# Three copies of split heads made by DMA, and the last sums completed block by block of tokens

## The chip, the cores and the metric

The kernel runs on one core of a Trainium2 chip. The metric is device time in microseconds (us) of one execution, as the median of several runs. The names of the engines are those of the profile: PE is TensorE (PEld its weight loads), DVE is VectorE, ACT is ScalarE, POOL is GpSimd, SP is SyncE, whose queue issues all the DMAs here. A name such as L233 is a line of the kernel before.

## The reference

Inputs are q, k, v of 8 batches x 8 heads x 576 tokens x 64 in float32, a memory matrix M_prev (64 x 64) and a vector z_prev (64) for each head, a gate beta for each head, and the weights of a feed-forward layer, 512 x 2048 and 2048 x 512. What is computed:

```python
scores = q @ k.T / sqrt(64)           # causal mask, 576 x 576 for each head
a = softmax(scores)
local = a @ v
q_p = elu(q) + 1
mem_out = (q_p @ M_prev) / (q_p . z_prev + 1e-6)
x = sigmoid(beta) * mem_out + (1 - sigmoid(beta)) * local
h = x.reshape(4608, 512) @ w_in
out = (h * sigmoid(h)) @ w_out        # 4608 x 512, float32
```

## The kernel before

**Precision.** A float32 number is split into a rounded part (type fp32r) and the rest ("high" and "low"), and a product is made as high x high + high x low + low x high in fp32r matmuls. The first ten heads (`N_WHOLE`) are "whole" instead: their attention runs in plain float32 matmuls. The other 54 heads are "split", and only these hold the three copies that the change touches.

**A head.** `scores` (from L215) transposes 64 channels of k and q together into `tt` (L221: k on partitions 0 to 63, q on 64 to 127). In a split head the two operands of the score product are built so that one pass over 128 partitions makes two terms:

- `kk`: rounded k above (L230, ACT), its rest below (L232, POOL).
- `qq`: rounded q on partitions 64 to 127 (L231, ACT) and once more on partitions 0 to 63 (L233, ACT); `ql` and 64 further columns of `qq` hold the rest of q (L235, POOL).
- L237 (ACT) repeats the last 64 columns of rounded q, on all 128 partitions, in 64 columns at the end of `qq`. They serve the second half of the last row of blocks (L274), which takes the columns S to S + 127 of `qq`.

The five blocks of 128 queries then follow: the score matmuls (L250; L274 for the last, of 64 queries in two halves), mask and minimum on DVE (L252, L284), the exponential on ACT (L254, L294), sums, and the normalizing of the probabilities `p` on POOL (L304). L307 (POOL) copies a 64 x 64 piece of the last block's probabilities to 64 columns further right, on the same partitions. The second transpose of L393 in each head reads that piece.

`values` (from L337) runs one head later: it transposes the probabilities on PE (L376, L384, L393), splits them (`ph` on ACT at L406, `pl` on DVE at L407) and multiplies by v and by the memory (L414, L422); the result goes into `xt`.

**The feed-forward part.** `ffn` works on 18 units of 256 tokens. A unit runs through eight pairs of blocks of the inner dimension: products into `h` (L552), tanh and the gating (L563, L564), the split into `g` (L567, L569), and, one pair later, the second product into two sums `acc` of 128 tokens each (`second`, L525 to L536). Within `second` the loop over the two weight tiles of the pair is the outer one and the loop over the two blocks of tokens the inner one; a block takes three matmuls from each tile. After the last pair the sums are scaled by 0.5 on ACT (L579) and stored (L581).

**Weights.** Most weight tiles stay on the chip. Twelve of the 32 ("flow": four of the first matrix, eight of the second) are read again for each unit (L485) into a ring of two buffers. Of the last pair of a unit the first tile stays on the chip and the second is a flow tile.

**The order of the work.** The main loop steps the generators for attention, weight preparation and feed-forward in turn, so that feed-forward steps lie between attention steps. The framework's planner then writes each engine's order of instructions by simulating the program with its own durations. On the chip each engine, and each queue of DMAs, runs its list strictly in order. Buffers set how far a head may run ahead: `tt`, `kk`, `qq` and the probabilities have two each, `raw` has one.

Of the kernel before, what the change touches and what calls it, by code (L numbers as in the profile page):

```python
# [12 lines left out]
AF = mybir.ActivationFunctionType  # L13
ALU = mybir.AluOpType
# [26 lines left out]
def memory_attention_then_silu_ffn(ctx, tc, q, k, v, M_prev, z_prev, beta, w_in, w_out, out):  # L41
    nc = tc.nc
    B, H, S, D = q.shape
    NT, DM = out.shape
    DFF = w_in.shape[1]
    P = 128
    NQ = (S + P - 1) // P
    LAST = S - (NQ - 1) * P
    SPLIT = 2 * P
    HI = S - SPLIT  # L50
    T = 256
    NU = NT // T
    KD = DM // P
    KF = DFF // P
    NP = KF // 2
# [17 lines left out]
    def f(ap):  # L73
        return ap.bitcast(F32)
# [11 lines left out]
        out=mask[:, 3 * P:], in_=mask[:, 3 * P:], pattern=[[-1, P]], base=0, channel_multiplier=1,  # L86
# [128 lines left out]
    def scores(b, h, raw, rest, made, whole):  # L215
# [4 lines left out]
        tt = pool.tile([P, S], F32, tag="tt", name="tt", bufs=NB["tt"])  # L220
        anchor["dve"] = nc.vector.transpose(out=tt, in_=raw.rearrange("p c e -> p (c e)")).ins  # L221
        if whole:
            qq = pool.tile([P, S], F32, tag="kk", name="qf", bufs=QK_BUFS)
            nc.scalar.copy(qq[0:64], tt[64:P])
            terms = [(qq[0:64], tt[0:64])]
        else:
            kk = pool.tile([P, S], F32R, tag="kk", name="kk", bufs=QK_BUFS)
            qq = qrow[h % QK_BUFS]
            ql = qlow[h % QK_BUFS]
            nc.scalar.copy(kk[0:64], tt[0:64])  # L230
            nc.scalar.copy(qq[64:P, 0:S], tt[64:P])  # L231
            nc.gpsimd.tensor_tensor(out=kk[64:P], in0=tt[0:64], in1=f(kk[0:64]), op=ALU.subtract)  # L232
            nc.scalar.copy(qq[0:64, 0:S], tt[64:P])  # L233
            for low, x0, x1 in ((ql[0:64], 0, S - LAST), (qq[0:64, S:S + LAST], S - LAST, S)):
                nc.gpsimd.tensor_tensor(  # L235
                    out=low, in0=tt[64:P, x0:x1], in1=f(qq[64:P, x0:x1]), op=ALU.subtract)
            nc.scalar.copy(qq[:, S + LAST:], f(qq[:, S - LAST:S]))  # L237
            terms = [(qq, kk), (ql, kk)]
        yield

# [4 lines left out]
        for i in range(NQ - 1):  # L245
            w = P * i + P
            pt = pool.tile([P, w], F32, tag=f"p{i}", name=f"p{i}", bufs=P_BUFS)
# [14 lines left out]
        pt = pool.tile([P, 3 * P], F32, tag=f"p{i}", name=f"p{i}", bufs=P_BUFS)  # L262
        halves = []
        for side, other, x0, x1, o in ((slice(0, LAST), slice(LAST, P), 0, SPLIT, P),
# [7 lines left out]
            else:  # L272
# [3 lines left out]
                if x1 == S:  # L276
                    nc.gpsimd.tensor_tensor(
                        out=row[:, x1 - x0 - LAST:], in0=row[:, x1 - x0 - LAST:], in1=mask[side, 4 * P - LAST:],
# [8 lines left out]
        def halves_of(out, src, op):  # L287
# [12 lines left out]
            out=st[:, 15:15 + NQ], in0=st[:, 10:10 + NQ], scalar=1.0e-9, in1=over[:, 1, h],  # L300
            op0=ALU.add, op1=ALU.mult)
# [2 lines left out]
            nc.gpsimd.tensor_scalar(  # L304
                pb[x], pb[x], st[:, 15 + x:16 + x], 1.0, op0=ALU.mult, op1=ALU.mult)
        if not whole:
            nc.gpsimd.tensor_copy(pt[LAST:P, HI:], pt[LAST:P, HI - LAST:HI])  # L307
        yield


# [1 line left out]
        if not whole:  # L312
            a, c = (D, 0) if odd else (0, D)
# [15 lines left out]
            out=r, in0=e, in1=zb.rearrange("p (o d) -> p o d", o=1).to_broadcast([P, NQ, D]), op=ALU.mult)  # L329
        nc.vector.tensor_reduce(nrm, r, axis=AX.X, op=ALU.add)  # L330
        nc.vector.scalar_tensor_tensor(
            out=nrm, in0=nrm, scalar=1.0e-6, in1=over[:, 0, h], op0=ALU.add, op1=ALU.mult)
        nc.vector.reciprocal(nrm, nrm)
        nc.gpsimd.tensor_tensor(
            out=e, in0=e, in1=nrm.rearrange("p (c o) -> p c o", o=1).to_broadcast([P, NQ, D]), op=ALU.mult)
# [143 lines left out]
    def flow():  # L479
        if flow_order:  # L480
            while flow_order[0] not in ready:
                yield "prepare"
            x = flow_order.pop(0)
            t = weight_tile(*x)
            nc.sync.dma_start(out=f(t), in_=scratch[x])  # L485
            flowing.append((x, t))

    def fetch(kind, c):
        if (kind, c) not in FLOW:
            return weight[kind, c]  # L490
        x, t = flowing.pop(0)
        assert x == (kind, c)
        return t

    def split_x(u):
        xu = []
        for kk in range(KD):
            t = pool.tile([P, 2, T], F32R, tag="xu", name="xu", bufs=XU_BUFS)
            t0 = u * T
            while t0 < (u + 1) * T:  # L500
                b = t0 // S
                n = min((b + 1) * S, (u + 1) * T) - t0
                src, o = xt[b, kk][:, t0 - b * S:t0 - b * S + n], t0 - u * T
                nc.scalar.copy(t[:, 0, o:o + n], src)
                nc.vector.tensor_tensor(out=t[:, 1, o:o + n], in0=src, in1=f(t[:, 0, o:o + n]), op=ALU.subtract)
                t0 += n
            xu.append(t)
        return xu

    def heads_needed(u):  # L510
        return ((u + 1) * T - 1) // S * H + H

    def ffn():
        ahead = None
        for _ in range(FLOW_BUFS):
            yield from flow()
        for u in range(NU):
            while done[0] < heads_needed(u):
                yield "wait"
            xu = ahead or split_x(u)  # L520
            ahead = None
            bank, tag = (ps_s, "s") if done[0] == B * H and u % 2 else (ps_a, "a")
            acc = [bank.tile([P, DM], F32, tag=tag, name="acc") for _ in range(T // P)]

            def second(p, g):  # L525
                for c in range(2):
                    w = fetch("o", 2 * p + c)
                    for t in range(T // P):
                        at = slice(t * P, (t + 1) * P)
                        terms = [(g[:, gi, c, at], w[:, wi]) for gi, wi in ((0, 0), (0, 1), (1, 0))]  # L530
                        for n, (ta, tb) in enumerate(terms):
                            nc.tensor.matmul(  # L532
                                acc[t], ta, tb, start=p == 0 and c == 0 and n == 0,
                                stop=p == NP - 1 and c == 1 and n == len(terms) - 1)
                    if ("o", 2 * p + c) in FLOW:
                        yield from flow()  # L536

            before = None
            for p in range(NP):
                while not {("i", 2 * p), ("i", 2 * p + 1)} <= ready:  # L540
                    yield "prepare"
                if done[0] == B * H and p % 2:
                    h = ps_t.tile([P, 2, T], F32, tag="t", name="h")
                else:
                    h = ps_h.tile([P, 2, T], F32, tag="h", name="h")
                for c in range(2):
                    w = fetch("i", 2 * p + c)
                    w4 = w.rearrange("p a (k f) -> p a k f", f=P)
                    for kk in range(KD):
                        terms = [(w4[:, wi, kk], xu[kk][:, xi]) for wi, xi in ((0, 0), (0, 1), (1, 0))]  # L550
                        for n, (ta, tb) in enumerate(terms):
                            nc.tensor.matmul(  # L552
                                h[:, c], ta, tb, start=kk == 0 and n == 0,
                                stop=kk == KD - 1 and n == len(terms) - 1)
                    if ("i", 2 * p + c) in FLOW:
                        yield from flow()
                yield
                if before:
                    yield from second(*before)

                h = h.rearrange("p c t -> p (c t)")
                th = pool.tile([P, 2 * T], F32, tag="row", name="th", bufs=ROW_BUFS)
                nc.scalar.activation(th, h, AF.Tanh, scale=0.5)  # L563
                nc.vector.scalar_tensor_tensor(out=th, in0=th, scalar=1.0, in1=h, op0=ALU.add, op1=ALU.mult)  # L564
                g = pool.tile([P, 2, 2, T], F32R, tag="g", name="g", bufs=G_BUFS)
                hi, lo = (g[:, j].rearrange("p c t -> p (c t)") for j in range(2))
                nc.scalar.copy(hi, th)  # L567
                late = nc.vector if done[0] == B * H else nc.gpsimd
                late.tensor_tensor(out=lo, in0=th, in1=f(hi), op=ALU.subtract)  # L569
                while not {("o", 2 * p), ("o", 2 * p + 1)} <= ready:  # L570
                    yield "prepare"
                before = p, g
                if p == NP - 2 and u + 1 < NU and done[0] >= heads_needed(u + 1):
                    ahead = split_x(u + 1)
                yield
            yield from second(*before)
            for t in range(T // P):
                o = pool.tile([P, DM], F32, tag="row", name="o", bufs=ROW_BUFS)
                nc.scalar.activation(o, acc[t], AF.Copy, scale=0.5)  # L579
                r0 = u * T + t * P  # L580
                nc.sync.dma_start(out=out[r0:r0 + P, :], in_=o)  # L581
            yield
# [53 lines left out]
```

## Time and profile before

| what | value |
|---|---|
| median of 3 runs | 1313.89 us (1313.21 to 1319.55) |
| the profiled execution, its own time | 1315.66 us |
| its span, first to last instruction | 1313.9 us |
| mean granted TensorE clock | 0.975 |
| busy share of PE / DVE / ACT / POOL | 96% / 68% / 67% / 63% |
| moved by DMA, mean rate | 190.39 MB, 145 GB/s |
| ACT, L233 and L237, 54 each | 36.3 and 12.9 us |
| POOL, L307, 54 | 13.5 us |

Busy time is the union of an engine's instructions. Matmuls are pipelined, so their durations overlap, and a busy PE isn't PE at its peak. The span falls into three stages: to about 195 us the whole heads and the splitting of the weights; to about 1117 us the split heads with feed-forward products between them; and the rest, feed-forward alone. A line of waits reads: who waited, for whom, us in total, times, longest.

### The profile page before, as it was taken

The numbers are of one execution on the slowest core, as the hardware profiler recorded it, in microseconds if no ns is written. First come the engines' busy times: TensorE is split into PE (matmuls) and PEld (weight loads), VectorE is DVE, ScalarE is ACT, GpSimd is POOL, SyncE is SP. The second block draws the span as 40 slices with busy tenths as digits, with TensorE's granted clock in tenths as the row PEclk, the third lists the DMA queues.
The fourth block names the chain that finished last, engine by engine and source line by source line (L and its number), as shares of the span: only waits on it lengthen the run. The fifth ranks groups of instructions, "written<-read, shape, count | busy, mean of one in ns | idle before, by whom it ended". The sixth has DMA issues, their size and how long they took to land.

```text
span 1313.9 us, 24653 instructions
## 1 busy us (share of the span) xinstructions
PE 1266.3 (96%) x7858; PEld 1084.0 (83%) x7858; DVE 898.1 (68%) x2472; ACT 884.5 (67%) x2143; POOL 822.9 (63%) x1133
## 2 busy tenths in 40 slices
PE   6988999999999999999999999999999999999998
PEld 2343458888999989998988989899898998999997
DVE  7988875778777777787767777777877775332222
ACT  6777866777787777777777777787878774322222
POOL 6878995777777777777777777767767763000000
PEclk9987779999999999999999999999999999999999
DMA  6766555555455555555555555555545432444444
GB/s 165 188 184 168 162 134 164 144 131 146 125 145 147 138 153 138 150 131 149 137 137 143 145 138 154 137 137 136 158 129 156 123 123 81 145 154 149 152 156 143
DMA packets 302994, 190.39 MB, mean 145 GB/s; under 512 B 258832, under 2 KB 267024, under 8 KB 302864
## 3 DMA queue, kind: packets, MB, share of 16 engines
q1 hardware_dynamic: 302864, 188.82, 51.9%
q8 instruction: 62, 1.02, 0.3%
q14 instruction: 68, 0.56, 0.1%
HBM read 173.02 MB, written 15.73 MB: 144 GB/s over the span
## 4 chain that ended last, share of the span: by engine, by line
PE 73%; DVE 11%; ACT 6%; issue 3%; POOL 3%; DMA 3%; SPq 1%; POOLq 0%; DVEq 0%; ACTq 0%
PE h L552 28%; PE acc L532 25%; PE x L422 7%; PE s L250 5%; PE tp L376 4%; PE tq L351 1%; PE x L414 1%; DVE s L252 1%; DVE wy L159 1%; DVE pl L407 1%; DVE st L290 1%; ACT p L254 1%; POOL p L304 1%; PE s L274 1%; DVE wy L154 1%
## 5 line engine op out<-in xcount | busy, mean ns | idle before, releaser
L552 PE MATMUL h<-xu,wi 128*128 128x256 f32 x2592 | 376.8, 287 | 8.7 <-DVE th L564 6.1
L552 PEld LDWEIGHTS h<-xu,wi 128*128 128x128 f32 x2592 | 343.0, 191 | 24.6 <-DVE th L564 7.8
L532 PE MATMUL acc<-wo,g 128*128 128x512 f32 x864 | 243.0, 398 | 0.0
L532 PE MATMUL acc<-flow,g 128*128 128x512 f32 x864 | 231.0, 394 | 0.5 <-DMA flow<-wo_s 0.5
L304 POOL TENSOR_SCALAR p<-p,st 128x384 f32<-128x384 f32 (+3 forms) x320 | 182.8, 592 | 75.3 <-DVE st L302 72.2
L564 DVE SCALAR_TENSOR_TENSOR th<-th,h 128x512 f32<-128x512 f32 x144 | 98.2, 683 | 143.5 <-ACT th L563 141.7
L532 PEld LDWEIGHTS acc<-flow,g 128*128 128x128 f32 x864 | 158.8, 188 | 33.6 <-DMA flow<-wo_s 1.0
L254 ACT ACTIVATE p<-s,st 128x128 f32<-128x128 f32 (+3 forms) x256 | 134.9, 528 | 69.9 <-DVE st L252 52.8
L569 POOL TENSOR_TENSOR g<-th,g 128x512 fp32r<-128x512 f32 x108 | 140.2, 1298 | 48.7 <-ACT g L567 46.9
L532 PEld LDWEIGHTS acc<-wo,g 128*128 128x128 f32 x864 | 149.1, 189 | 18.9 <-POOL p L304 0.5
L563 ACT ACTIVATE th<-h 128x512 f32<-128x512 f32 x144 | 85.9, 597 | 99.7 <-PE h L552 97.4
L407 DVE TENSOR_TENSOR pl<-tp,ph 128x384 fp32r<-128x384 f32 x216 | 118.5, 551 | 34.6 <-ACT ph L406 31.3
L252 DVE CUSTOM_DVE_ANT_0 s<-s,mask 128x128 f32<-128x128 f32 (+3 forms) x256 | 125.3, 491 | 23.1 <-PE s L250 19.6
L567 ACT CAST g<-th 128x512 fp32r<-128x512 f32 x144 | 89.2, 620 | 53.0 <-DVE th L564 52.1
L376 PE MATMUL tp<-ident,p 128*128 128x128 f32 x640 | 121.8, 291 | 3.2 <-POOL p L304 2.5
L552 PE MATMUL h<-xu,flow 128*128 128x256 f32 x864 | 122.6, 283 | 0.0
L406 ACT CAST ph<-tp 128x384 fp32r<-128x384 f32 x216 | 104.7, 490 | 26.1 <-PE x L422 21.2
L552 PEld LDWEIGHTS h<-xu,flow 128*128 128x128 f32 x864 | 112.8, 191 | 1.9 <-issue 0.3
L376 PEld LDWEIGHTS tp<-ident,p 128*128 128x128 f32 x640 | 82.2, 148 | 28.6 <-POOL p L304 9.0
L422 PE MATMUL x<-pl,vs 128*128 128x256 f32 x324 | 82.1, 308 | 0.9 <-DVE pl L407 0.9
L232 POOL TENSOR_TENSOR kk<-tt,kk 64x576 fp32r<-64x576 f32 x54 | 77.4, 1432 | 5.0 <-ACT kk L230 1.2
L422 PE MATMUL x<-ph,vs 128*128 128x320 f32 (+4 forms) x378 | 78.2, 275 | 1.4 <-POOL vs L316 0.8
(104 smaller groups left out, 2409.5 us busy)
## 6 DMA issues: line engine op xcount, KB each, us to landing
flow<-wo_s SPq DMA_DIRECT2D x144, 512.0 KB, 3.6
flow<-wi_s SPq DMA_DIRECT2D x72, 512.0 KB, 3.8
raw<-in_k SPq DMA_DIRECT2D x128, 72.0 KB, 2.5
raw<-in_q SPq DMA_DIRECT2D x128, 72.0 KB, 2.7
out<-o SPq DMA_DIRECT2D x36, 256.0 KB, 4.2
wraw<-in_moe_w_in SPq DMA_DIRECT2D x16, 512.0 KB, 4.4
qn<-in_q SPq DMA_DIRECT2D x64, 128.0 KB, 2.9
vr<-in_v SPq DMA_DIRECT2D x64, 128.0 KB, 2.5
```

The costliest lines, as they stand in the source:

```text
L252: anchor["dve"] = nc.vector.tensor_tensor_reduce(s, s, mask[:, 3 * P - P * i:], QS, 3.0e38, ALU.add, ALU.min, st[:, i:i + 1]).ins
L254: nc.scalar.activation(pt, s, AF.Exp, bias=st[:, i:i + 1], scale=-1.0, accum_out=st[:, 10 + i:11 + i])
L304: nc.gpsimd.tensor_scalar(pb[x], pb[x], st[:, 15 + x:16 + x], 1.0, op0=ALU.mult, op1=ALU.mult)
L376: nc.tensor.transpose(t[:, o:o + P], pb[i][:, P * j:P * j + P], ident)
L406: nc.scalar.copy(ph[:, 0:o], t[:, 0:o])
L407: nc.vector.tensor_tensor(out=pl[:, 0:cut], in0=t[:, 0:cut], in1=f(ph[:, 0:cut]), op=ALU.subtract)
L422: nc.tensor.matmul(x[0:rows, q0:n], vs[0:n_k, j], part[0:n_k, o:o + n - q0], start=False, stop=last)
L532: nc.tensor.matmul(acc[t], ta, tb, start=p == 0 and c == 0 and n == 0, stop=p == NP - 1 and c == 1 and n == len(terms) - 1)
L552: nc.tensor.matmul(h[:, c], ta, tb, start=kk == 0 and n == 0, stop=kk == KD - 1 and n == len(terms) - 1)
L564: nc.vector.scalar_tensor_tensor(out=th, in0=th, scalar=1.0, in1=h, op0=ALU.add, op1=ALU.mult)
L567: nc.scalar.copy(hi, th)
L569: late.tensor_tensor(out=lo, in0=th, in1=f(hi), op=ALU.subtract)
```

## The change

Three copies of a split head become DMAs on SP's queue. Copy one takes rounded q from partitions 64 to 127 of `qq` to partitions 0 to 63 (so it reads what L231 wrote, where ACT had cast `tt` a second time). Copy two repeats the last 64 columns on all 128 partitions; it reads what copy one and L231 wrote. Copy three is that of the last probabilities.

In the very last call of `second` (last unit, last pair) both weight tiles are fetched first and the loop over the blocks of tokens becomes the outer one: the first block's sum gets its six matmuls, then the second block's. In the last unit the second block is scaled on DVE instead of ACT.

```diff
@@ scores
-            nc.scalar.copy(qq[0:64, 0:S], tt[64:P])
+            nc.sync.dma_start(out=f(qq[0:64, 0:S]), in_=f(qq[64:P, 0:S]))
...
-            nc.scalar.copy(qq[:, S + LAST:], f(qq[:, S - LAST:S]))
+            nc.sync.dma_start(out=f(qq[:, S + LAST:]), in_=f(qq[:, S - LAST:S]))
...
-            nc.gpsimd.tensor_copy(pt[LAST:P, HI:], pt[LAST:P, HI - LAST:HI])
+            nc.sync.dma_start(out=pt[LAST:P, HI:], in_=pt[LAST:P, HI - LAST:HI])
@@ second
+                def product(c, t, w):
+                    at = slice(t * P, (t + 1) * P)
+                    terms = [(g[:, gi, c, at], w[:, wi]) for gi, wi in ((0, 0), (0, 1), (1, 0))]
+                    for n, (ta, tb) in enumerate(terms):
+                        nc.tensor.matmul(
+                            acc[t], ta, tb, start=p == 0 and c == 0 and n == 0,
+                            stop=p == NP - 1 and c == 1 and n == len(terms) - 1)
+
+                if u == NU - 1 and p == NP - 1:
+
+                    both = [fetch("o", 2 * p + c) for c in range(2)]
+                    for t in range(T // P):
+                        for c in range(2):
+                            product(c, t, both[c])
+                    return
                 for c in range(2):
                     w = fetch("o", 2 * p + c)
                     for t in range(T // P):
-                        at = slice(t * P, (t + 1) * P)
...
+                        product(c, t, w)
@@ ffn
-                nc.scalar.activation(o, acc[t], AF.Copy, scale=0.5)
+                if u == NU - 1 and t % 2:
+                    nc.vector.tensor_scalar(o, acc[t], 0.5, None, op0=ALU.mult)
+                else:
+                    nc.scalar.activation(o, acc[t], AF.Copy, scale=0.5)
```

More of the change, by code (lines that the diff above doesn't have):

```diff
@@ L528, in second @@
                     for t in range(T // P):
-                        at = slice(t * P, (t + 1) * P)
[L530 to L534, printed above, removed]
+                        product(c, t, w)
                     if ("o", 2 * p + c) in FLOW:
```

## The prediction, made before the result was known

> **What bounds the kernel now.** I read the page first, then a table of busy time by stage, then TensorE's own waits, and then the places that the change touches. From the page:
>
> ```profile
> span 1313.9 us, 24653 instructions
> PE 1266.3 (96%) x7858; PEld 1084.0 (83%) x7858; DVE 898.1 (68%) x2472; ACT 884.5 (67%) x2143; POOL 822.9 (63%) x1133
> ```
>
> TensorE is busy 96% of the span, the next engine 68%. The stages say more (columns: stretch, its length, then busy time and instruction count of PE, PEld, DVE, ACT, POOL, the granted clock, the DMA share, GB/s):
>
> ```profile
> 100.00:200.00 100.00, 90.77 (x321) 48.28 (x322) 81.43 (x187) 75.77 (x182) 92.67 (x88) 0.73 0.58 159
> 700.00:800.00 100.00, 98.81 (x677) 91.32 (x676) 73.03 (x222) 76.93 (x191) 73.80 (x110) 1.00 0.52 140
> 1200.00:1314.00 114.00, 109.65 (x689) 98.63 (x687) 29.19 (x45) 29.17 (x51) 0.00 (x0) 1.00 0.45 148
> ```
>
> In the middle stage PE is busy 98.8 of 100 us, while ACT, which the change relieves, has 23 us free in it. In the last stage only the feed-forward products run, and the other engines are nearly idle. What is still to be had in the middle is the list of PE's waits from 195 to 1117 us, which is whole here:
>
> ```profile
> PE h L552 <- DVE th L564: 5.8, 10, 1.0
> PE s L250 <- ACT p L254: 4.0, 7, 0.8
> PE x L422 <- DVE pl L407: 0.9, 2, 0.6
> PE x L422 <- POOL vs L316: 0.8, 1, 0.8
> PE x L414 <- DVE xt L430: 0.6, 2, 0.3
> PE tp L376 <- DVE pl L407: 0.5, 2, 0.3
> PE x L422 <- ACT ph L406: 0.5, 1, 0.5
> PE s L274 <- ACT p L254: 0.2, 1, 0.2
> ```
>
> Together 13.3 us of 922, or 1.0% of the span. No DMA stands among them. So the kernel is bound by TensorE's own work, which the change leaves as it is, and 13.3 us is the most that the three copies can win in this stage.
>
> The Trainium skill warns against just this reading: its page "Perfetto Trace Analysis", section "Identifying the Most-Contended Engine", says that matmul busy time is no measure of headroom and that the busy share of weight loads is a better one. By that rule the middle stage has 8.7 us free in each 100 (PEld 91.3), some 80 us in all. The trace does not bear that out: in the last stage, where PE waits for almost nothing, PEld is lower still (98.63 of 114 us, 87%). I go by the list of waits.
>
> **The three copies: what goes.** The groups by form:
>
> ```profile
> L233 ACT CAST qq<-tt 64x576 fp32r<-64x576 f32 x54 | 36.3, 672 | 1.3
> L237 ACT CAST qq<-qq 128x64 fp32r<-128x64 f32 x54 | 12.9, 239 | 0.1
> L307 POOL COPY p<-p 64x64 f32<-64x64 f32 x54 | 13.5, 250 | 3.4
> ```
>
> Each runs once for each of the 54 split heads; the first ten heads are whole and keep theirs. ACT loses 672 + 239 = 911 ns a head, 49.2 us; POOL loses 250 ns a head, 13.5 us. None of it is PE's time. The split heads are about 17 us apart (54 in some 920 us), so six pass in 100 us and ACT falls from 76.9 to about 71.4.
>
> What is that worth? Of the 13.3 us all but the 0.8 us behind POOL go back, through DVE or directly, to something that ACT makes (th, p, ph, xb): 12.5 us. If such lateness grows like busy over free time, it goes from 76.9/23.1 = 3.3 to 71.4/28.6 = 2.5, a quarter less: **3.0 us** won. This is an estimate from those rows. The bounds are 0, if it is DVE's own queue that is late (the largest wait ends on a DVE instruction), and 12.5 us, if ACT alone sets them. POOL's two points I count at nothing: it is 74% busy and ends 0.8 us of waits.
>
> **What comes: latency.** The nearest issues, with size and time to landing:
>
> ```profile
> raw<-in_q SPq DMA_DIRECT2D x128, 72.0 KB, 2.7
> mr<-in_M_prev SPq DMA_DIRECT2D x128, 16.0 KB, 2.2
> zb<-in_z_prev SPq DMA_DIRECT2D x64, 32.0 KB, 3.4
> ```
>
> The new transfers are 144 KB (64 partitions by 576 words), 32 KB (128 by 64) and 16 KB (64 by 64). No SBUF to SBUF transfer is in the trace. By these rows I take 2.7, 2.7 and 2.2 us; bounds 2.2 and 3.4. So the first copy lands 2.0 us later than ACT's 0.67 us made it, the second, which reads what the first wrote, some 4.5 us later, the third 2 us later. Whether anybody waits is seen by counting. ACT's row, and then how many casts and score matmuls had started by three times (the whole heads have 80 of L250, each split head 8):
>
> ```profile
> 604.29 0.67 ACT L233 CAST qq<-tt 64x576 fp32r<-64x576 f32 x1
> 0.00:607.50 607.50, 18.15 (x27) 0.95 0.57 151
> 0.00:625.00 625.00, 96.67 (x288) 50.84 (x288) 0.95 0.57 151
> 0.00:626.00 626.00, 97.09 (x290) 51.14 (x290) 0.95 0.57 151
> ```
>
> The copy at 604.29 is the 27th. The 27th head's first matmul is number 80 + 26 x 8 + 1 = 289, and it starts after 625. So there are 20 us between the copy and its first reader: copies one and two cost **nothing**, hidden by the earlier head's work that PE still has before it. Were that cover gone, 2.0 us a head would be 108 us. The third copy, in the same way (POOL's L307, then L393, of which the whole heads have 20 and each split head 2, the second reading the copied columns):
>
> ```profile
> 0.00:619.00 619.00, 6.50 (x25) 0.95 0.57 151
> 0.00:631.00 631.00, 20.98 (x69) 10.92 (x70) 0.95 0.57 150
> ```
>
> The 25th copy is there by 619, and its reader is matmul 70, after 631: 12 us of cover for 2.2 us. At the first split heads, before this lead has built up, I allow up to 1 us.
>
> **What comes: SyncE's queue.** All three go to SP, which issues in order, so what stands behind them waits too: for ACT's L231, for the first copy's landing, and for POOL's L304. Issue time, landing and waits from 195 to 1117 us:
>
> ```profile
> L209 SPq DMA_DIRECT2D mr<-in_M_prev x102: 465/547/597, 203.2 to 1043.5; - x102
> DMA to landing us min/median/max: 3.1/3.8/5.4
> SPq L193 <- DVE tt L221: 49.1, 16, 6.5
> SPq L201 <- ACT qp L358: 20.5, 14, 2.4
> SPq L485 <- DMA flow<-wo_s: 3.1, 2, 2.9
> ```
>
> The second line belongs to the flow weights of L485. Three issues of 0.55 us are 1.6 us a head. The loads that matter are these flow weights, with two buffers and 163 loads in this stage, three a head. One of them, and its reader:
>
> ```profile
> 603.73 0.53 SPq L485 DMA_DIRECT2D flow<-wo_s  x1
> 613.44 1.54 PE L532 MATMUL acc<-flow,g 128*128 128x512 f32 x6
> ```
>
> From issue to use are 9.7 us, less 3.8 for the landing: 5.9 us to spare. One hold of 2.7 us for the first copy's landing fits, as does a wait of 2.4 us for ACT. I count **0**; below it the end is also 0 (a later load wins nothing), above it the queue rival's price.
>
> **The order.** A planner with its own durations writes each engine's order, so past the tenth head the rows change places, and the trace cannot say how. The list above is what one such order costs. Another may have it all once more (+13.3) or nothing of it; I take no mean shift.
>
> **The last sums.** The end of the trace (the timelines of PE, ACT and SP, then the size and landing of the last flow load), and DVE's group with a pass over as much:
>
> ```profile
> 1305.75 1.64 PE L532 MATMUL acc<-flow,g 128*128 128x512 f32 x6 [0.52 <-DMA flow<-wo_s]
> 1307.23 1.54 PE L532 MATMUL acc<-wo,g 128*128 128x512 f32 x6
> 1308.61 1.56 PE L532 MATMUL acc<-flow,g 128*128 128x512 f32 x6
> 1309.57 1.29 ACT L579 ACTIVATE o<-acc 128x512 f32<-128x512 f32 x2 [3.65 <-PE acc L532]
> 1303.89 0.32 SPq L485 DMA_DIRECT2D flow<-wo_s  x1
> flow<-wo_s SPq DMA_DIRECT2D x1, 512.0 KB, 4.5
> L569 DVE TENSOR_TENSOR g<-th,g 128x512 fp32r<-128x512 f32 x36 | 24.9, 694 | 22.4 <-ACT g L567 22.3
> ```
>
> Now six matmuls read the resident tile (1.38 us from 1307.23 to 1308.61) and six the last flow tile. In the new order the flow tile is wanted after three, at 1307.9. It was issued at 1303.89 and took 4.5 us: it lands at 1308.4, so PE stands about **0.5 us**; before, the landing came 0.2 us ahead of the use. The second block's scaling goes from ACT (0.60) to DVE; a pass over as much there takes 0.69: +0.1. The first block's scaling no longer stands ahead of it, but it was through when PE ended (1309.57 + 0.60 = 1310.17), so that wins nothing; the first output leaves 1 us sooner, perhaps 0.1 us for the second. Sum +0.5 us; bounds -0.3 (tile in time, outputs apart) and +0.7.
>
> **The sum.** -3.0 + 0 + 0 + 0 + 0.5 = -2.5 us. The profiled execution took 1315.66 us, 1313.9 of span and 1.8 around it; it goes to 1313.2. The median of the runs is 1313.89, 1.8 below that execution, so I forecast **1311.4** there. About 0.5% (6.6 us) is what a measurement of this kernel can tell from no change: it would be called the same.
>
> **The rivals.**
>
> A, ACT sets PE's waits. For it: th, p and ph are ACT's, and ACT is the fuller of those whose load falls. Against: the largest item ends on DVE, whose load stays. All 12.5 us go: 1313.9 - 12.5 + 0.5 = 1301.9. It counts as faster from a gain of 6.6, half the list. Chance 0.24.
>
> B, SP's queue becomes the bound. Place: the flow load issued behind the copies. The holds add up to 2.7 (landing) + 1.6 (issues) + 2.4 (ACT) = 6.7 us where all fall between two flow loads; that is 0.8 over the spare, and a flow load with only 3 us to spare would be 3.7 late. At 3 us in one head of five, 11 x 3 = 33 us less the 2.5: 1344; in one of fifteen it is 1322. It decides from three such loads among the 163 (9 us, against the gain of 2.5 and the 6.6 that can be told). Against: SP has long waits already (6.5 us on DVE's transposes) and PE's list has no DMA. Chance 0.10.
>
> The Trainium skill makes the hold necessary: "DMA: Bandwidth & Descriptors", section "Two DMAs through the same engine are not ordered", says that the issuing engine has to wait for the first transfer's semaphore before a second that reads its result. The wait of 2.9 us of L485 on a DMA above shows such a hold here.
>
> C, the new order is worse for PE: the list twice, 1313.9 + 13.3 - 2.5 = 1324.7. The point is 9 us more of it. Chance 0.07.
>
> D, nothing of ACT's relief reaches PE: 1314.4, the tail alone. Chance 0.12; the forecast has 0.47.
>
> **Range and chances.** A reaches to 1301.9 and B's mild form to 1322: 1302 to 1321 leaves out B's and C's upper parts and A's lowest. Faster: A's 0.24 and 0.03 of the forecast's; slower: B and C, 0.17; same: the remaining 0.56.
>
> **What would show it.** ACT some 49 us and POOL 13 us less busy, with L233, L237 and L307 gone and three rows on SP of 54 each, landing in 2.2 to 3.4 us. PE's list from 195 on about 10 us, with no DMA on it: right; a "DMA qq" ahead of L250 or L274 breaks the count of 20 us, a "DMA flow" of several us in the middle is B. At the end a wait of L532 of about 0.5 us for the flow tile. Wrong if the middle stage's time for the same heads moves by over 7 us.

## The result, and the profile after

The change makes the kernel slower: 1328.66 us median against 1313.55, a ratio of 1.0106 (95% interval 1.0084 to 1.0129), 15 us. The forecast was 1311.4 and its range ended at 1321.

What the change does to the engines goes the way that was forecast. The page, then the row of the middle stage, and the new transfers with size and time to landing:

```profile
span 1329.7 us, 24959 instructions
PE 1281.4 (96%) x7858; PEld 1086.0 (82%) x7858; DVE 911.2 (69%) x2473; ACT 843.2 (63%) x2034; POOL 812.9 (61%) x1079
```

```profile
700.00:800.00 100.00, 98.66 (x669) 89.64 (x668) 75.01 (x220) 70.77 (x172) 70.51 (x101) 1.00 0.58 151
```

```profile
qq<-qq SPq DMA_DIRECT2D x54, 144.0 KB, 3.1
...
qq<-qq SPq DMA_DIRECT2D x54, 32.0 KB, 1.8
...
p<-p SPq DMA_DIRECT2D x54, 16.0 KB, 2.2
```

ACT is 41.3 us less busy and POOL 10.0, where 49 and 13 were forecast; DVE is 13.1 us busier with one instruction more, which nothing here explains. Yet TensorE does its unchanged work more slowly: for the same 7858 matmuls its busy time has gone from 1266.3 to 1281.4 us, so over the whole span the page counts most of the lost time as matmul and not as waiting. The share of PE's busy time from 700 to 800 us hardly tells it (98.8 and 98.7); the count of matmuls does. From 300 to 1100 us, a stretch of split heads in both kernels, first before, then after (PE, PEld, DVE, ACT, POOL, then clock, DMA share, GB/s):

```profile
300.00:1100.00 800.00, 788.42 (x5356) 725.23 (x5356) 601.38 (x1779) 609.40 (x1510) 584.65 (x859) 1.00 0.52 140
```

```profile
300.00:1100.00 800.00, 781.39 (x5252) 712.46 (x5251) 613.79 (x1769) 568.63 (x1411) 570.09 (x799) 1.00 0.56 149
```

104 matmuls fewer, at 800 / 5356 = 0.149 us each in the mean, are 15.5 us by this estimate: the loss is here. The clock is a small part of it. Before, the granted clock reads 1.00 in every stretch of 100 us from 200 us on. After, it was halved once between 200 and 1300 us, right after PE had stood 1.48 us for `th`:

```profile
614.48 1.78 PE L562 MATMUL h<-xu,wi 128*128 128x256 f32 x7 [1.48 <-DVE th L574]
```

```profile
614.50:618.00 3.50, 3.50 (x17) 3.50 (x18) 1.90 (x5) 2.86 (x7) 2.68 (x4) 0.51 0.78 263
```

3.5 us at half the clock cost 1.7 us by this estimate. Whether the wait brought it about isn't shown. PE's list of waits after, from 195 to 1130 us, its longer rows:

```profile
PE h L562 <- DVE th L574: 3.5, 4, 1.5
PE x L422 <- POOL vs L316: 2.9, 3, 1.6
PE tq L351 <- DVE ph L410: 1.8, 2, 1.3
...
PE tq L351 <- ACT o L592: 1.4, 1, 1.4
PE tp L376 <- DVE pl L407: 1.4, 3, 0.6
PE tp L376 <- POOL p L304: 1.3, 3, 0.6
...
PE acc L530 <- DMA flow<-wo_s: 0.9, 3, 0.5
```

(L562, L574 and L530 are L552, L564 and L532 of before.) The list has grown from 13.3 to 18.7 us, and its rows are others: the products of `values` (tq, tp, x) now wait for what POOL, DVE and ACT make. The flow weights are 0.9 us of it, so SP's queue isn't the bound. SP does hold:

```profile
SPq L237 <- DMA qq<-qq: 91.8, 43, 4.3
...
SPq L307 <- POOL p L304: 26.2, 23, 3.2
```

What has changed is seen where a head's probabilities are handed from POOL to PE. Before (POOL's timeline, then PE's):

```profile
614.74 2.63 POOL L304 TENSOR_SCALAR p<-p,st 128x128 f32<-128x128 f32 x5 [0.82 <-DVE st L302]
...
625.09 0.49 PE L376 MATMUL tp<-ident,p 128*128 128x128 f32 x3
```

and after:

```profile
749.56 2.63 POOL L304 TENSOR_SCALAR p<-p,st 128x128 f32<-128x128 f32 x5
...
749.99 0.33 PE L376 MATMUL tp<-ident,p 128*128 128x128 f32 x1
...
751.69 0.44 PE L376 MATMUL tp<-ident,p 128*128 128x128 f32 x2 [0.35 <-POOL p L304]
...
753.09 0.44 PE L422 MATMUL x<-ph,vs 128*128 128x256 f32 x2 [0.36 <-POOL vs L316]
```

Before, the transposes start 7.7 us after POOL's last block (614.74 + 2.63 = 617.37, to 625.09). In the head shown of after, they start while POOL is still at the first blocks, and follow it block by block. That is so in 20 of the last 50 heads, and before in 2. Over these heads the median from the end of L304 to the first transpose has gone from 7.4 us to 1.1.

The programs themselves say the same. Compared instruction by instruction, the planner's order for the kernel with three DMAs (last sums as before) has moved a PE matmul by 24 places in the mean. The products of `values` stand 39 to 46 places earlier in the mean, the feed-forward products some 17 later.

### The profile page after: what moved, and what is told of

It is laid out like the page before. It is cut to its first block, busy times and chain, and to the rows that moved or that the text cites. A ratio compares the mean times of both kernels' runs of the same rounds, so it can differ in the third digit from the quotient of the medians.

```text
span 1329.7 us, 24959 instructions
## 1 busy us (share of the span) xinstructions
PE 1281.4 (96%) x7858; PEld 1086.0 (82%) x7858; DVE 911.2 (69%) x2473; ACT 843.2 (63%) x2034; POOL 812.9 (61%) x1079
## 5 line engine op out<-in xcount | busy, mean ns | idle before, releaser
L562 PE MATMUL h<-xu,wi 128*128 128x256 f32 x2592 | 376.9, 287 | 4.7 <-DVE th L574 3.5
L562 PEld LDWEIGHTS h<-xu,wi 128*128 128x128 f32 x2592 | 344.2, 191 | 19.2 <-issue 4.5
L530 PE MATMUL acc<-wo,g 128*128 128x512 f32 x864 | 241.0, 398 | 0.0
L530 PE MATMUL acc<-flow,g 128*128 128x512 f32 x864 | 234.7, 397 | 1.5 <-DMA flow<-wo_s 1.4
L304 POOL TENSOR_SCALAR p<-p,st 128x384 f32<-128x384 f32 (+3 forms) x320 | 188.2, 609 | 69.2 <-DVE st L302 61.0
L574 DVE SCALAR_TENSOR_TENSOR th<-th,h 128x512 f32<-128x512 f32 x144 | 98.4, 684 | 134.0 <-ACT th L573 132.7
L530 PEld LDWEIGHTS acc<-flow,g 128*128 128x128 f32 x864 | 157.6, 188 | 34.4 <-DMA flow<-wo_s 4.1
L530 PEld LDWEIGHTS acc<-wo,g 128*128 128x128 f32 x864 | 150.2, 189 | 21.3 <-issue 0.9
L376 PE MATMUL tp<-ident,p 128*128 128x128 f32 x640 | 126.0, 293 | 8.0 <-POOL p L304 3.7
L562 PE MATMUL h<-xu,flow 128*128 128x256 f32 x864 | 123.4, 286 | 0.0
L562 PEld LDWEIGHTS h<-xu,flow 128*128 128x128 f32 x864 | 112.2, 192 | 0.5 <-DMA flow<-wi_s 0.2
L235 POOL TENSOR_TENSOR ql<-tt,qq 64x512 fp32r<-64x512 f32 x54 | 69.6, 1288 | 43.8 <-ACT qq L231 20.7
```

Source lines behind the costliest of these rows:

```text
L304: nc.gpsimd.tensor_scalar(pb[x], pb[x], st[:, 15 + x:16 + x], 1.0, op0=ALU.mult, op1=ALU.mult)
L376: nc.tensor.transpose(t[:, o:o + P], pb[i][:, P * j:P * j + P], ident)
L530: nc.tensor.matmul(acc[t], ta, tb, start=p == 0 and c == 0 and n == 0, stop=p == NP - 1 and c == 1 and n == len(terms) - 1)
L562: nc.tensor.matmul(h[:, c], ta, tb, start=kk == 0 and n == 0, stop=kk == KD - 1 and n == len(terms) - 1)
```

## The experiments

The two theories: **order**, the loss is the order that the planner writes once the copies are DMAs; and **DMA**, it is what the DMAs do on the chip (SP held, landings waited for, more separate waits on PE). All ratios are to the kernel before, run beside it on the same chip.

**The parts one at a time.** Each of these is the kernel before with one edit of the change, planned afresh.

```diff
# e1: the edits in second() and in the scaling alone
# e2: copy one alone
-            nc.scalar.copy(qq[0:64, 0:S], tt[64:P])
+            nc.sync.dma_start(out=f(qq[0:64, 0:S]), in_=f(qq[64:P, 0:S]))
# e3: copy two alone
-            nc.scalar.copy(qq[:, S + LAST:], f(qq[:, S - LAST:S]))
+            nc.sync.dma_start(out=f(qq[:, S + LAST:]), in_=f(qq[:, S - LAST:S]))
# e4: copy three alone
-            nc.gpsimd.tensor_copy(pt[LAST:P, HI:], pt[LAST:P, HI - LAST:HI])
+            nc.sync.dma_start(out=pt[LAST:P, HI:], in_=pt[LAST:P, HI - LAST:HI])
```

> The kernel before with only the change of the last sums. Both theories (the copies' DMAs hold SP's queue; the planner's new order of all engines is worse) put the loss in the copies: 1313.5 to 1314.2 us, the tail's own part between -0.3 and +0.7 us.

> The kernel before with only copy one (rounded q to partitions 0 to 63) as a DMA. Queue theory: no other DMA's landing is waited for on SP, the waits of this row in the changed kernel were 18 us in all, so at most +3 us. Order theory: every engine's order is written anew from the first split head on, so the loss is unrelated to how much is moved; some +5 to +15 us are possible for this edit alone, or a gain.

> The kernel before with only copy two (the repeat of the last 64 columns) as a DMA; what it reads comes from ACT alone, so SP does not wait for a landing. Queue theory: at most +3 us, while copies one and two together cost most of the 15 us. Order theory: as for copy one, +5 to +15 us or a gain, in no proportion to the size.

> The kernel before with only copy three (the last probabilities) as a DMA. Queue theory: SP waits for POOL some 60 us in all in the changed kernel in this row, so up to +4 us. Order theory: as for copy one, +5 to +15 us or a gain.

| edit | median, us | ratio | 95% interval |
|---|---|---|---|
| last sums | 1315.20 | 0.9993 | 0.9976 to 1.0009 |
| copy one | 1346.22 | 1.0222 | 1.0188 to 1.0256 |
| copy two | 1329.78 | 1.0105 | 1.0071 to 1.0139 |
| copy three | 1315.47 | 0.9997 | 0.9977 to 1.0018 |

The kernel before took 1315.39 us beside them. The last sums and copy three cost nothing that can be told. Copy one alone costs 29 us, more than the whole change and more than either theory had: the parts don't add. So the loss is no price per transfer, and the plain queue theory is out (copy two alone, where SP waits for no landing, costs 14 us against 3 at most). The order moves the more, the larger the loss: copy three moves 19% of PE's matmuls, by 1.1 places in the mean; copy two 66%, by 7.7; copy one 80%, by 24. Copy one alone has a second trouble, which the next runs separate: copy two stands on ACT behind it and waits for its landing there.

**DMAs in the old order, and the old copies in the new order.** The planner's order can be taken from one program and given to another, since both trace the same instructions one for one (the code is shortened, and the comments are added here):

```diff
+    nc, order = build(arrays, copies_of_A)            # the planner's order for program A
     with tile.TileContext(nc, schedule_with_timeline_sim=True) as tc:
         memory_attention_then_silu_ffn(tc, *args)     # program B
+        for engine, names in order.items():
+            same = [traced[n] for n in names if str(traced[n].engine) == engine]
+            for first, then in zip(same, same[1:]):   # issue order only, no wait
+                tc.add_manual_dep(then, first.name, why, reason="order")
```

What is on another engine in B than in A is left for the planner to place. In the first run B has the three DMAs and A is the kernel before; in the second B is the kernel before and A has the three DMAs; in the third B has copy one as a DMA and A is the kernel before.

> All three copies as DMAs, last sums as before; but PE, DVE, ACT, POOL and SP are made to issue what they share with the kernel before in exactly its order (the DMAs are put between on SP where the planner finds them ready). Order theory (the loss is the planner's new order of the engines): the loss goes, 1311 to 1318 us against 1315 of before. DMA theory (SP held, landings waited for, more waits on PE): the loss stays, 1325 to 1332 us.

> The copies on ACT and POOL as before, no new DMA; but every engine issues what it shares with the three-DMA kernel in that kernel's order. Order theory: the loss comes without any DMA, 1325 to 1332 us. DMA theory: 1313 to 1318 us.

> Only copy one as a DMA (1346 us with the planner's order), the engines held to the order of the kernel before. Order theory: 1312 to 1318 us. DMA theory: most of the 31 us stay, over 1335 us.

| kernel | median, us | ratio | 95% interval |
|---|---|---|---|
| three DMAs, old order | 1310.47 | 0.9973 | 0.9954 to 0.9992 |
| old copies, new order on all engines | 1348.83 | 1.0250 | 1.0216 to 1.0283 |
| copy one as DMA, old order | 1383.17 | 1.0524 | 1.0506 to 1.0543 |

With the old order the same three DMAs make the kernel faster. The DMA theory is out for the three together, and the order theory holds. The second run goes the same way but overshoots 1332: its ACT issues in an order written for an ACT without two copies, so it may not be a clean price. That this is the reason isn't shown.

The third run contradicts the order theory as I had put it: 70 us slower than the kernel before, in its order. The waits of that kernel show why (L247 is copy two, still on ACT):

```profile
DVE th L577 <- ACT th L576: 135.0, 53, 8.1
ACT qq L247 <- DMA qq<-qq: 126.3, 45, 6.3
POOL g L582 <- ACT g L580: 97.2, 41, 7.7
```

ACT stands 126 us for copy one's landing, with th, ph and xb behind it. With the planner's order (the run with copy one alone) it had been:

```profile
ACT qq L237 <- DMA qq<-qq: 48.9, 33, 4.2
```

So where a landing is waited for decides. On SP the hold costs nothing that can be told (the run with three DMAs in the old order); on ACT `th`, `ph` and `xb` stand behind it.

**Only TensorE held; the whole change; copy two.** TensorE alone is held, in both directions; the whole change is run in the old order; and copy two alone.

```diff
# e8: program B with the three DMAs, only PE held to the old order
# e11: program B the kernel before, only PE held to the order for three DMAs
         for engine, names in order.items():
+            if engines and not any(e in engine for e in engines):    # engines = ('PE',)
+                continue
# e9: program B the whole change, A the kernel before with the new last sums; all engines held
# e10: program B with copy two as DMA, A the kernel before; all engines held
```

> All three copies as DMAs, and only TensorE held to the order of the kernel before; the planner orders the other engines and SP as it likes. In its own order for three DMAs it puts the products of values (x, tq) some 50 matmuls further ahead on PE. If that is the loss: 1308 to 1314 us, as with all engines held. If the loss is in the order of DVE, ACT, POOL or SP: over 1320 us.

> The whole change, last sums included, with every engine held to the order that the planner wrote without the DMAs. Order theory: 1310 to 1311 us, a ratio of about 0.997 and faster than both kernels. DMA theory: 1328 us as the changed kernel.

> Only copy two as a DMA (1.0105 with the planner's order), the engines held to the order of the kernel before. What it reads and what reads it have cover, and no compute engine other than PE waits for it. Order theory: 1311 to 1316 us, ratio 0.997 to 1.002. DMA theory: over 1324 us. If it is slow here, a copy by DMA whose neighbour is on ACT costs something of its own, as in the run with copy one alone.

> The copies on ACT and POOL as before, no new DMA, and only TensorE made to issue in the order that the planner writes for the three DMAs; the other engines are planned around that. If TensorE's order alone is the loss: 1324 to 1332 us, as the changed kernel. If the order is bad only together with the DMAs' landings or with SP's queue: 1311 to 1317 us.

| kernel | median, us | ratio | 95% interval |
|---|---|---|---|
| three DMAs, PE in the old order | 1313.34 | 0.9985 | 0.9971 to 0.9998 |
| whole change, old order | 1309.69 | 0.9960 | 0.9942 to 0.9979 |
| copy two as DMA, old order | 1315.91 | 1.0007 | 0.9992 to 1.0022 |
| old copies, PE in the new order | 1329.79 | 1.0107 | 1.0079 to 1.0136 |

This settles order against DMA. With every copy on ACT and POOL and no new DMA, PE in the new order costs 1.0107, as the changed kernel does (1.0106). Taking that order away with all three DMAs in place removes the loss. It does not settle which engine's order matters: the programs of these two runs show that the planner brings the other engines along with PE. With only PE held to the new order, ACT's instructions stand 0.1 places in the mean from that order and 4.8 from the old one, DVE's 0.5 and 4.5; with only PE held to the old order, it is the other way round. So what is shown is the order of the engines together. The matmuls from 300 to 1100 us, for the whole change in the old order and then for the old copies with PE in the new one:

```profile
300.00:1100.00 800.00, 791.79 (x5383) 728.73 (x5382) 605.89 (x1779) 572.76 (x1417) 570.07 (x810) 1.00 0.56 151
```

```profile
300.00:1100.00 800.00, 778.30 (x5237) 710.67 (x5236) 606.95 (x1766) 599.42 (x1496) 580.91 (x849) 1.00 0.51 137
```

Against 5356 before they are 27 more and 119 fewer. In the kernel with PE in the new order the median from the end of L304 to the first transpose is 1.1 us, and PE waits for POOL as it does after the change, for longer in all:

```profile
PE h L565 <- DVE th L577: 6.2, 7, 1.6
PE x L435 <- POOL vs L329: 5.2, 6, 1.8
PE tp L389 <- POOL p L314: 3.3, 3, 1.4
```

while the whole change in the old order has that median at 7.5 us and keeps the list of before, shorter, although SP is held longer by the landing of copy one (the last row, from SP's list):

```profile
PE h L576 <- DVE th L588: 4.7, 11, 0.8
PE s L261 <- ACT p L265: 2.8, 5, 0.8
```

```profile
SPq L246 <- DMA qq<-qq: 121.1, 48, 6.2
```

The whole change in the old order is faster than both kernels: by 0.4% against before (0.2% to 0.6%), some 5 us.

Copy two's 14 us go with the old order as well (1.0007), but the order that cost them is bad in another way. In the planner's order for copy two alone the products of `values` are moved back as often as ahead (less than one place in the mean), and the median from L304 to the first transpose is 6.8 us, close to the 7.4 of before. PE's longest rows there, and a row of 100 us in which 633 matmuls ran (680 before) at a clock of 0.97:

```profile
PE s L250 <- ACT p L254: 5.4, 8, 1.5
PE tp L376 <- DVE pl L407: 3.5, 6, 0.9
PE tp L376 <- DVE qp L359: 3.4, 3, 1.8
```

```profile
900.00:1000.00 100.00, 96.68 (x633) 88.47 (x632) 68.18 (x203) 68.82 (x168) 66.69 (x100) 0.97 0.51 134
```

So the closed gap behind POOL goes with the loss of the whole change, but it isn't what makes every new order bad, and no run changed it alone.

Open is why the planner puts the products of `values` ahead when copy one is a DMA: its durations stand in no trace, and nothing was run on that. How the 15.5 us fall on single waits isn't shown either; the lists leave most of the loss out.

## Why the prediction was wrong

**What failed is the step "The order".** It said that the rows change places, that the trace cannot say how, and took no mean shift with a bound of 13.3 us; the bad case was rival C, 1324.7 us at a chance of 0.07. Rival C had the mechanism, with 11 us over the kernel before. The measured price of the new order is 15.5 us with the old copies (10 to 18 by the interval, so the bound isn't excluded there), and some 19 between the two orders of the whole change (1.0106 and 0.9960 of before; 15 to 23 from the two intervals). So the middle value was wrong, and for the whole change the bound too. The measure failed with them: "The list above is what one such order costs" took PE's waits for the price, but the list grew by only 5.4 us (13.3 to 18.7) where the kernel lost 15, and so the list before bounds nothing.

**"What comes: latency" failed with it as a forecast, not as an arithmetic.** The 20 and 12 us of cover were read rightly from the old order, and there they hide the DMAs: with the three DMAs and the old order there is no loss. But a cover that one order leaves is no property of the kernel. The new order put the products of `values` close behind POOL, and 7.4 us between POOL's probabilities and their first transposes became 1.1.

**The three copies' gain agrees with the runs, once the order is held.** The sum had 3.0 us. In the old order the three DMAs gain 0.27% (0.08% to 0.46%), 1.1 to 6.0 us, and PE's list there falls from 13.3 to 10.7 us, where about 10 was forecast. ACT stands at 72.6 of 100 us in the middle stage there, against 71.4 forecast and 76.9 before. That ACT's relief is what gains was not tested by itself. Rival A, all 12.5 us, isn't borne out.

**SyncE's queue, and rival B.** Zero agrees with the runs. SP is held 121 us by copy one's landing in the fastest kernel, and PE's list has no more than 0.9 us of flow weights after the change. The wait that the Trainium skill's page "DMA: Bandwidth & Descriptors", section "Two DMAs through the same engine are not ordered", makes necessary is there on SP in every run in which copies one and two are both DMAs (91.8 us of SP's time in the changed kernel). Its cost depends on its place: nothing measurable on SP, and 126 us of ACT's time where the second copy stayed on ACT and waited there for the first one's landing.

**The last sums.** Forecast +0.5 us with bounds of -0.3 and +0.7; measured 0.9993 (0.9976 to 1.0009, or -3.2 to +1.2 us, which can't tell 0.5 us from nothing). But the profile after shows that the step's reading was wrong. PE's timeline at its end (x5 on the resident tile, then three on the flow tile):

```profile
1322.96 1.30 PE L530 MATMUL acc<-wo,g 128*128 128x512 f32 x5
...
1324.10 0.85 PE L530 MATMUL acc<-flow,g 128*128 128x512 f32 x3
...
1324.79 0.39 PE L530 MATMUL acc<-wo,g 128*128 128x512 f32 x1
...
1325.02 0.85 PE L530 MATMUL acc<-flow,g 128*128 128x512 f32 x3
```

The planner doesn't keep the order of the source: it put two matmuls of the second block ahead of the flow tile's first, so no wait for that tile is recorded. The step took the order of the source for the order on the chip: the same mistake as above, on a small scale.

**The bound from busy time.** I set aside the rule of the Trainium skill's page "Perfetto Trace Analysis", section "Identifying the Most-Contended Engine", that weight loads tell headroom better than matmul busy time. For the loss it was the better guide: of the estimated 15.5 us, PE's busy time from 300 to 1100 us shows 7.0 (788.42 to 781.39), PE's list of waits grew by 5.4, and the weight loads show 12.8 (725.23 to 712.46). As a measure of the level my objection stands: in the last stage, which hardly waits, the loads are at 87%.

## What to carry to other kernels

Where a planner writes the order of the engines, an edit that moves a small operation to another queue is two edits: the operation, and a new order for everything behind it; the second can be several times the first (here a loss of 14 to 19 us against a gain of 1 to 6). Test them apart by giving one program the other's order, and if the edit is good in the old order, keep that order with it. And count the matmuls over a long stretch of like work: from 300 to 1100 us their number fell by 1.9%, PE's busy time by 0.9%.

## What was not expected of the hardware

In the changed kernel a copy of 144 KB from SBUF to SBUF took 3.1 us to landing, 32 KB took 1.8 and 16 KB 2.2, so the smallest wasn't the fastest. The size doesn't set it alone: the same 32 KB copy took 2.8 and 2.9 us in the two runs in which it was the only one of the three made by DMA. With the order held, a DMA's landing waited for on ACT cost 70 us in 54 heads (1.3 us each), where the wait on SP cost nothing that could be measured. Part of the 70 us is a lower clock, 0.98 against 1.00 from 300 to 1100 us: 2% of 800 us, some 16 us by this estimate.
